# Cutting the first weight load in two, and loading x and c by their eight real rows, in a decode step that streams 165 MB

## The chip, the cores and the metric

The kernel runs on one core of a Trainium2 chip. A core has a matrix engine (TensorE, "PE" in the profile, with its weight loads as "PEld"), a vector engine (VectorE, "DVE"), a scalar engine (ScalarE, "ACT"), GpSimd ("POOL") and SyncE ("SP"), and 16 DMA engines that move data between the chip's main memory and the core's tile memory of 128 rows (partitions). SP and ACT both issue DMAs here, each on a queue of its own (q1 for SP and q10 for ACT in the profile). The metric is device time in microseconds (us) from start to end of the program: 394.66 us before, the median of three runs (394.59 to 395.08).

## The reference

One decode step of a transformer block for a batch of 8 with adaptive layer norm. `x` and `c` are both 8 rows of 512 numbers; the rest are weights and a key and value cache, all in 32-bit floats:

```
mod = (silu(c) @ w_mod).reshape(8, 6, 1, 512)         # w_mod: 512 x 3072
sa, ca, ga, sb, cb, gb = six parts of mod
h = layernorm(x) * (1 + ca) + sa
x = x + ga * attention(h, k_cache, v_cache, wq, wo)   # last 2048 keys of 8192
h = layernorm(x) * (1 + cb) + sb
x = x + gb * mlp(h, w1, b1, w2, b2)                   # relu squared, 512 -> 1792 -> 512
```

The attention has 32 query heads of 128 numbers on 8 key/value heads. For each of the 8 batch rows and 8 heads, 2048 keys and 2048 values of 128 floats are read: 134 MB of the 165 MB in all.

## The kernel before, in words

**Loads.** Nearly everything passes through five big tiles in the tile memory: four of 128 rows by 8192 floats ("big", 4096 KB each) and one half as wide ("small"). The list `loads` fixes the order: `w_mod` in two pieces (mod 0 into a big tile and mod 1 into the small one), `wq` in two, K 0, K 1, and then a K and a V piece in turn, with `wo` in between, and `w1` and `w2` last. `pump()` issues the next load of the list on SP's queue as soon as a tile of its size is free, and `done(...)` frees a tile after its last reader and calls `pump()` again. Mod 0, mod 1, wq 0, wq 1 and K 0 need no tile to come free, so they are all issued at the start; K 1 waits until the matmuls on mod 0 (L270) have let go of its tile, K 2 for those on wq 0 (L296), and so on. Each load is one DMA whose row r of 128 goes to row r of the tile. The branch for `w_mod` is at L113 to L116; a row of mod 0 is 8192 floats in one piece, 32 KB.

**x and c.** The host lays x and c out as one array of 128 x 2 x 128: the 512 columns in four groups q, each at rows 32q to 32q+7 for the eight batch rows, and zeros in the other 24 rows of each group. L64 loads it on ACT's queue, 128 rows of 1 KB, into `xc_in`.

**The head.** silu of c (L193 to L196, on ACT and DVE) and its transpose give `cT` (L189, L198). Layer norm's sums go over `xc_in` (L214 to L228) and PE adds up the four groups with the matrix `sel` (L216, L223). Then PE does `cT` times mod 0 and mod 1 (L270), DVE finishes h (L281 on), PE does the queries (L296, L311).

**The main loop** runs 32 steps over K and V pieces: DVE transposes keys (L182), PE makes scores (L351), softmax runs on ACT and DVE, PE adds up values (L440). **The tail** is the projection, the second norm and the MLP with `w1` (L603) and `w2` (L622), and the store of the output (L632).

The order on each engine is that of the program text (a manual schedule), and every engine runs its list in order. Waits are on semaphores that are placed automatically. DMAs take their completion semaphores in rotation from a set of eight, and a DMA that takes one whose last user is still under way waits for that user first.

Of the kernel before, what the change touches and what calls it, by code (L numbers as in the profile page):

```python
# [19 lines left out]
def tile_adaln_cached_attention_mlp(  # L20
# [14 lines left out]
    nc = tc.nc  # L35
    P = 128
    B, HKV, SK, DH = k_cache.shape
    D = wq.shape[0]
# [22 lines left out]

    xc_in = consts.tile([P, 2, P], F32, name="xc_in")
    x_in, c_in = xc_in[:, 0, :], xc_in[:, 1, :]
    nc.scalar.dma_start(xc_in, xc)  # L64

    ident = consts.tile([P, P], F32, name="ident")
    make_identity(nc, ident)
# [7 lines left out]
    big = NJ * DH  # L75
# [8 lines left out]
    def size_of(key):  # L84
        return "small" if key[0] in ("wo", "w1") or key == ("mod", 1) else "big"

    def load(key):
        kind, i = key
        held[key] = free[size_of(key)].pop(0)
        t = slots[size_of(key)][held[key]]  # L90
        if kind in "KV":

            hk, c = divmod(i, 2)
            v = k_cache[4 * c : 4 * c + 4, hk] if kind == "K" else v_cache[c::2, hk]
            v = v[:, SK - W :, :].rearrange("u (p j) d -> p u (j d)", j=NJ)
            cuts = (0, big // 2, big * 3 // 4, big) if key == ("V", 2 * HKV - 1) else (0, big)
            for x, y in zip(cuts, cuts[1:]):
                nc.sync.dma_start(t[:, x:y], v[..., x:y])
            return

        def rows(o, v):
            n = v.shape[1] * v.shape[2]
            nc.sync.dma_start(t[:, o : o + n].rearrange("p (a n) -> p a n", n=v.shape[2]), v)

        def wo_rows(j):

            r = 2 * REP * DH
            return wo[j * r : (j + 1) * r, :].rearrange("(h p i) n -> p h (i n)", p=P, i=4)

        w1v = w1.rearrange(r_kc, p=P)  # L110
        if kind == "wo":
            rows(0, wo_rows(i))
        elif kind == "mod":  # L113

            v = w_mod.rearrange("(p kc) n -> p (kc n)", p=P)
            nc.sync.dma_start(t, v[:, big:] if i else v[:, :big])  # L116
        elif kind == "wq":

            nc.sync.dma_start(t, wq.rearrange("(p h a) n -> h p (a n)", p=P, h=2)[i])
        elif kind == "tail":  # L120
            for h in range(2):
                rows(h * 4 * D, wo_rows(HKV // 2 - 1)[:, h : h + 1])
            rows(big // 2, w1v[:, 0:2])
        elif kind == "w1":
            rows(0, w1v[:, 2:4])
        else:
            v = w2.rearrange("(p c) n -> p c n", p=P)
            for lo, hi in ((0, 8), (8, 10), (10, 12), (12, 13), (13, 14)):
                rows(D * lo, v[:, lo:hi])
# [14 lines left out]
    def pump():  # L144
        while at[0] < len(loads) and free[size_of(loads[at[0]])]:
            load(loads[at[0]])
            at[0] += 1
# [356 lines left out]
    for s in range(N + PV_LAG + 1):  # L504
        g, i = divmod(s, C)
        q, h = divmod(s, 2)
        v = s - PV_LAG
# [104 lines left out]
    r = work.tile([P, FC, B], F32, name="relu", tag="a", bufs=1)  # L612
# [56 lines left out]
```

## Time and profile before

| what | value |
|---|---|
| median of three runs | 394.66 us |
| span of the profiled execution | 392.6 us |
| moved by DMA | 165.12 MB, mean 421 GB/s |
| PE busy | 256.3 us, 65% of the span |
| DVE busy | 218.1 us, 56% |
| ACT busy | 46.1 us, 12% |

The profiled execution is given by its span alone, from its first to its last recorded instruction; the median of the runs is 2.1 us above it, which is what lies around the span and the spread between executions. Times in rows of the profile count from the span's start. "DMA share" in a table of windows is the time of the packets that began in the window, over the 16 DMA engines, so a short window can show more than 1. A releaser in a row ("idle <- X") is what ended an engine's wait.

### The profile page before, as it was taken

The numbers are of one execution on the slowest core, as the hardware profiler recorded it, in microseconds if no ns is written. First come the engines' busy times: TensorE is split into PE (matmuls) and PEld (weight loads), VectorE is DVE, ScalarE is ACT, GpSimd is POOL, SyncE is SP. The second block draws the span as 40 slices with busy tenths as digits, with TensorE's granted clock in tenths as the row PEclk, the third lists the DMA queues.
The fourth block names the chain that finished last, engine by engine and source line by source line (L and its number), as shares of the span: only waits on it lengthen the run. The fifth ranks groups of instructions, "written<-read, shape, count | busy, mean of one in ns | idle before, by whom it ended". The sixth has DMA issues, their size and how long they took to land.

```text
span 392.6 us, 4672 instructions
## 1 busy us (share of the span) xinstructions
PE 256.3 (65%) x2006; PEld 80.7 (21%) x2006; DVE 218.1 (56%) x322; ACT 46.1 (12%) x89; POOL 1.3 (0%) x8
## 2 busy tenths in 40 slices
PE   0173869668328873797375827883775837994996
PEld 0121200122002321133021202220222211332433
DVE  1370299959056845774582817780776457855231
ACT  1200101410003100310031003010201003004010
POOL 0000000000000000000000000000000000000000
PEclk9999789988958995989699888997788959897899
DMA  8999999999999999999999999999999999999994
GB/s 329 432 425 436 444 437 437 431 426 402 454 427 427 426 427 431 429 441 430 437 423 431 427 436 427 429 431 431 407 447 427 436 431 438 426 419 412 428 423 169
DMA packets 7908, 165.12 MB, mean 421 GB/s; under 512 B 840, under 2 KB 1104, under 8 KB 1616
## 3 DMA queue, kind: packets, MB, share of 16 engines
q1 hardware_dynamic: 7728, 164.70, 98.2%
q8 instruction: 15, 0.25, 0.3%
q10 hardware_dynamic: 160, 0.14, 0.1%
q14 instruction: 5, 0.04, 0.0%
HBM read 164.77 MB, written 0.07 MB: 420 GB/s over the span
## 4 chain that ended last, share of the span: by engine, by line
DMA 65%; DVE 17%; PE 13%; issue 4%; SPq 0%; DVEq 0%
DMA big<-in_A_k_cache_dram 47%; DVE kT L182 9%; DMA big<-in_A_wq_dram 7%; DMA big<-in_A_wo_dram 6%; DMA big<-in_B_w_dram 5%; PE s_ps L351 5%; DVE pT L419 4%; PE p_ps L384 3%; PE o_ps L440 2%; DVE pr L412 2%; DVE mx L365 1%; PE m_ps L296 1%; PE m_ps L367 1%; PE m_ps L389 1%; DVE o_sb L458 1%
## 5 line engine op out<-in xcount | busy, mean ns | idle before, releaser
L182 DVE STREAM_TRANSPOSE kT<-big 128x1024 f32<-128x1024 f32 x128 | 151.7, 1221 | 90.2 <-DMA big<-in_A_k_cache_dram 86.1
L351 PE MATMUL s_ps<-kT,qst 128*32 128x512 f32 x512 | 130.1, 1076 | 19.8 <-DVE kT L182 19.7
L440 PE MATMUL o_ps<-big,pT 128*32 128x256 f32 x1024 | 73.0, 410 | 2.1 <-DMA big<-in_A_v_cache_dram 1.1
L440 PEld LDWEIGHTS o_ps<-big,pT 128*32 128x32 f32 x1024 | 35.3, 120 | 85.0 <-issue 69.5
L367 PE MATMUL m_ps<-ident,mx 128*1 128x128 f32 x16 | 4.3, 365 | 59.9 <-DVE mx L365 59.9
L351 PEld LDWEIGHTS s_ps<-kT,qst 128*32 128x32 f32 x512 | 16.4, 118 | 38.4 <-DVE kT L182 28.4
L419 DVE STREAM_TRANSPOSE pT<-pr 128x2048 f32<-128x2048 f32 x8 | 18.2, 2273 | 1.0 <-ACT pr L402 1.0
L402 ACT ACTIVATE pr<-pr,own 128x512 f32<-128x512 f32 x16 | 17.8, 1218 | 0.3
L396 ACT ACTIVATE pr<-p_ps,nm 128x512 f32<-128x512 f32 x8 | 5.5, 688 | 95.9 <-DVE nm L393 95.9
L339 ACT COPY qst<-q_ps 32x128 f32<-32x128 f32 x32 | 8.2, 257 | 72.0 <-PE q_ps L328 71.7
L361 ACT COPY ss<-s_ps 128x512 f32<-128x512 f32 x8 | 4.7, 586 | 99.5 <-issue 71.4
L296 PE MATMUL m_ps<-big,h1T 128*32 128x512 f32 x64 | 10.1, 790 | 8.5 <-DMA big<-in_A_wq_dram 8.5
L464 PE MATMUL m_ps<-o_sb,pick 128*128 128x256 f32 x16 | 6.1, 466 | 14.4 <-DVE o_sb L458 14.4
L367 PEld LDWEIGHTS m_ps<-ident,mx 128*1 128x1 f32 x16 | 0.7, 80 | 65.1 <-DVE mx L365 65.1
L314 DVE COPY qbd<-m_ps 32x128 f32<-32x128 f32 x8 | 3.0, 372 | 18.1 <-PE m_ps L311 18.0
L384 PE MATMUL p_ps<-ss,perm 128*128 128x512 f32 x16 | 11.9, 839 | 0.0
L216 PE MATMUL m_ps<-xsum,sel 128*128 128x1 f32 x2 | 0.6, 363 | 16.9 <-DVE xsum L214 16.9
L393 DVE COPY nm<-m_ps 128x1 f32<-128x1 f32 x8 | 1.3, 158 | 18.5 <-PE m_ps L389 18.5
L412 DVE TENSOR_SCALAR pr<-pr,own 128x512 f32<-128x512 f32 x16 | 9.2, 654 | 0.8 <-ACT pr L396 0.8
L457 DVE TENSOR_SCALAR o_sb<-o_ps,bit 128x128 f32<-128x128 f32 x16 | 4.9, 306 | 7.7 <-PE o_ps L440 7.7
L423 PE MATMUL m_ps<-zs,tsel 128*128 128x8 f32 x16 | 2.9, 252 | 8.9 <-DVE zs L414 8.9
L464 PEld LDWEIGHTS m_ps<-o_sb,pick 128*128 128x128 f32 x16 | 2.6, 203 | 25.9 <-DVE o_sb L458 25.9
(124 smaller groups left out, 119.8 us busy)
## 6 DMA issues: line engine op xcount, KB each, us to landing
big<-in_A_k_cache_dram SPq DMA_DIRECT2D x16, 4096.0 KB, 28.8
big<-in_A_v_cache_dram SPq DMA_DIRECT2D x15, 4096.0 KB, 20.9
big<-in_A_wq_dram SPq DMA_DIRECT2D x2, 4096.0 KB, 32.1
small<-in_A_wo_dram SPq DMA_DIRECT2D x3, 2048.0 KB, 26.6
big<-in_w_mod_dram SPq DMA_DIRECT2D x1, 4096.0 KB
small<-in_w_mod_dram SPq DMA_DIRECT2D x1, 2048.0 KB, 17.1
big<-in_A_v_cache_dram SPq DMA_DIRECT2D x1, 2048.0 KB, 21.5
big<-in_A_v_cache_dram SPq DMA_DIRECT2D x2, 1024.0 KB, 21.2
```

The costliest lines, as they stand in the source:

```text
L182: nc.vector.transpose(KTS[q, j][:, rows], k[:, rows, 32 * j : 32 * j + 32])
L296: nc.tensor.matmul(pqs[r][32 * g : 32 * g + 32, :], hT[:, kc, :], w[:, 4 * r + g, :], start=(kc == 0), stop=(kc == NQ - 1),)
L339: nc.scalar.copy(own[b, :, :, i, 0], pq[b, :P].rearrange("p (c m t) -> p c m t", c=2, t=REP))
L351: nc.tensor.matmul(s_ps[0][32 * g : 32 * g + 32, :], qst[hk % 2][:, P * (4 * c + u) + 32 * j :][:, :32], kT[:, u], start=(c == 0 and j == ...
L367: nc.tensor.matmul(MX_[hk][0:1, :P], mx, ident, start=True, stop=True)
L384: nc.tensor.matmul(sp, perm, SS_.pop(hk), start=True, stop=True)
L396: nc.scalar.activation(pr.rearrange("p j x -> p (j x)"), SS_.pop(hk), AF.Exp, bias=nm, scale=SCALE, accum_out=z)
L402: nc.scalar.mul(X_[hk][..., w], pr, own[:, w : w + 1])
L412: nc.vector.tensor_scalar(X_[hk][..., w], pr, own[:, w : w + 1], None, op0=ALU.mult)
L419: nc.vector.transpose(PT_[hk].rearrange("p e j r -> p j e r"), X_.pop(hk).rearrange("p j x w -> p j (x w)"))
L440: nc.tensor.matmul(O_[n][32 * g : 32 * g + 32, : 2 * DH], PT_[hk][:, e, j : j + 2].rearrange("p j r -> p (j r)"), vt[:, j : j + 2, :].rear ...
L464: nc.tensor.matmul(pp[:, : 2 * DH], pick.rearrange("p t u -> p (t u)"), o.rearrange("p e d -> p (e d)"), start=True, stop=True)
```

## The change

Two edits. The load of x and c becomes a clearing of the whole tile on DVE and then four DMAs of 8 rows each, on the same queue as before. The load of mod 0 becomes two DMAs on SP's queue, of its first 16 rows and of the other 112; mod 1 stays one DMA.

```diff
     xc_in = consts.tile([P, 2, P], F32, name="xc_in")
     x_in, c_in = xc_in[:, 0, :], xc_in[:, 1, :]
-    nc.scalar.dma_start(xc_in, xc)
+    nc.vector.memset(xc_in, 0.0)
+    for q in range(D // P):
+        nc.scalar.dma_start(xc_in[32 * q : 32 * q + B], xc[32 * q : 32 * q + B])
...
             v = w_mod.rearrange("(p kc) n -> p (kc n)", p=P)
-            nc.sync.dma_start(t, v[:, big:] if i else v[:, :big])
+            for r in (slice(0, P),) if i else (slice(0, 16), slice(16, P)):
+                nc.sync.dma_start(t[r], v[r, big:] if i else v[r, :big])
```

In the lists of instructions that the two programs build, SP has one DMA more, ACT three more and DVE one memset more, ahead of all its other work. The rotation of the eight semaphores moves by four places. That places new waits near the start: on SP, the load of wq 1 waits until the 16-row piece has landed, and that of K 0 until the first load of x and c has; on ACT, the load of the activation table ahead of L193 waits for the other three loads of x and c, and all four of these wait for the memset. From K 1 on, each load waits for the same earlier loads as before or for ones of the start, and in the tail every wait has its counterpart.

## The prediction

> **What bounds the kernel now.** I read the page first, for the share of DMA, then the table of windows by stage, then the start in order of time, then the last links of the chain.
>
> ```profile
> span 392.6 us, 4672 instructions
> ...
> PE 256.3 (65%) x2006; PEld 80.7 (21%) x2006; DVE 218.1 (56%) x322; ACT 46.1 (12%) x89; POOL 1.3 (0%) x8
> ...
> q1 hardware_dynamic: 7728, 164.70, 98.2%
> q8 instruction: 15, 0.25, 0.3%
> q10 hardware_dynamic: 160, 0.14, 0.1%
> ...
> DMA 65%; DVE 17%; PE 13%; issue 4%; SPq 0%; DVEq 0%
> ```
>
> No engine is busy over 65%, but SP's queue q1 keeps all 16 DMA engines at work for 98.2% of the span. Its rate is 164.70 MB over 16 x 392.6 x 0.982 us = 26.7 GB/s for one engine, so a 32 KB row of mod 0 costs an engine 32,768 / 26,700 = 1.23 us. The next table (time, busy time of each engine, clock, DMA share, GB/s) shows whether the stream ever pauses.
>
> ```profile
> 1.50:3.50 2.00, 0.00 (x0) 0.00 (x0) 0.75 (x6) 0.96 (x1) 0.00 (x0) 1.00 0.96 262
> 3.50:12.50 9.00, 0.00 (x0) 0.00 (x0) 0.00 (x0) 0.00 (x0) 0.00 (x0) 1.00 0.98 421
> 12.50:42.00 29.50, 15.78 (x116) 5.35 (x120) 10.55 (x42) 2.88 (x7) 0.00 (x0) 0.93 1.03 441
> 42.00:384.00 342.00, 235.37 (x1779) 72.14 (x1772) 205.95 (x271) 41.98 (x81) 0.47 (x1) 0.86 1.00 429
> 384.00:392.60 8.60, 5.14 (x116) 3.19 (x114) 0.60 (x3) 0.00 (x0) 0.00 (x0) 1.00 0.35 135
> ```
>
> From 1.5 us to 384 us it doesn't: the share is 0.96 to 1.03 in each stretch. The chain's last links say that the end follows the last load at once:
>
> ```profile
> 346.09 22.87 DMA big<-in_A_wo_dram
> ...
> 369.03 19.87 DMA big<-in_B_w_dram
> ...
> 388.94 0.47 PE m_ps L622 x8
> ```
>
> So the span is a start of about 1.75 us, one unbroken stream, and some 4 us behind it. Whatever makes the stream start earlier, shrinks it or slows it anywhere moves the end by as much; what compute does early is covered as long as SP issues each load before the stream has used up those ahead of it. That cover is large at the start:
>
> ```profile
> 0.73 0.42 ACTq L64 DMA_DIRECT2D xc_in<-in_xc_dram  x1
> ...
> 0.73 0.39 SPq L116 DMA_DIRECT2D big<-in_w_mod_dram  x1
> ...
> 1.18 0.42 SPq L116 DMA_DIRECT2D small<-in_w_mod_dram  x1
> 1.18 1.28 ACT L193 ACT_TABLE_LOAD   x1 [1.18 <-PEq L655]
> ...
> 13.54 0.31 ACT L193 ACTIVATE e_sb<-xc_in 128x128 f32<-128x128 f32 x1 [11.08 <-DMA xc_in<-in_xc_dram]
> ...
> 18.80 6.40 PE L270 MATMUL m_ps<-big,cT 128*32 128x512 f32 x40
> ```
>
> ```profile
> 25.27 0.54 SPq L98 DMA_DIRECT2D big<-in_A_k_cache_dram  x1
> ```
>
> ```profile
> DMA to landing us min/median/max: 33.2/35.5/46.1
> ```
>
> The last row is for L98's first loads: K 0, issued at 2.68 us, is the longest, 46.1 us, and lands at 48.8 us. K 1 is issued at 25.27 us, when the tile of mod 0 is free. The head could thus run 48.8 - 25.3 = 23.5 us later before the stream stood still, and running earlier gains nothing.
>
> **The 16-row piece.** How rows and engines go together is seen in half-microsecond windows (same columns):
>
> ```profile
> 1.00:1.50 0.50, 0.00 (x0) 0.00 (x0) 0.17 (x1) 0.32 (x1) 0.44 (x2) 1.00 0.00 0
> 1.50:2.00 0.50, 0.00 (x0) 0.00 (x0) 0.40 (x3) 0.50 (x1) 0.00 (x0) 1.00 2.73 721
> 2.00:2.50 0.50, 0.00 (x0) 0.00 (x0) 0.35 (x3) 0.46 (x1) 0.00 (x0) 1.00 0.73 197
> 2.50:3.00 0.50, 0.00 (x0) 0.00 (x0) 0.00 (x0) 0.00 (x0) 0.00 (x0) 1.00 0.37 131
> 3.00:3.50 0.50, 0.00 (x0) 0.00 (x0) 0.00 (x0) 0.00 (x0) 0.00 (x0) 1.00 0.00 0
> 3.50:4.00 0.50, 0.00 (x0) 0.00 (x0) 0.00 (x0) 0.00 (x0) 0.00 (x0) 1.00 1.29 545
> 4.00:4.50 0.50, 0.00 (x0) 0.00 (x0) 0.00 (x0) 0.00 (x0) 0.00 (x0) 1.00 1.25 537
> ```
>
> What begins from 1.5 to 3.0 us is 0.5 x (721 + 197 + 131) = 524 KB, 16 rows of 32 KB, one on each engine; then nothing until the next 16 rows at 3.5 to 4.5 us. A 128-row load is thus 16 equal streams of 8 rows each. The 16-row piece gives all 16 engines one row each, too, but all of them in one corner of the tile. If the ways into the tile memory belong to rows, as the even split of 128 rows over 16 streams suggests but doesn't show, these 16 rows share few ways. Bounds: with 16 ways the piece takes 1.23 us, as before; with eight neighbouring rows to a way it has two ways and takes 8 x 1.23 = 9.84 us, a loss of 8.6 us. No row here shows a load of few rows with weight, so I choose between the ends: four ways, in the lower half of the steps 2, 4, 8, 16, because the simplest cut of 128 rows into 16 streams keeps neighbours together. That is 4 x 1.23 = 4.92 us, a loss of **3.7 us** (an estimate; 0 to 8.6). Behind it on each engine stand its rows of the 112-row piece, so nothing covers the loss.
>
> [...]
>
> **The 112 rows.** Seven rows to an engine, 7 x 1.23 = 8.6 us if they never meet. But 112 rows no longer fall on the ways in the even pattern: with 16 ways of 8 rows, the ways that the first piece left alone have 8 rows to take, 9.84 us, so 1.2 us is lost even if all runs smoothly; at worst an engine stands behind another one's row four times, 4 x 1.23 = 4.9 us. Without shared ways it is 0. I take **1.2 us**, since the streams queue ahead and can even out.
>
> **An earlier start.** The first wave is slow: from 1.5-2.0 to 3.5-4.0 us is 2.0 us instead of 1.23, and the sixteen rows begin up to a microsecond apart. If that comes from SP setting up 128 rows at once, a small first piece takes up to 0.8 us off; if it is the delay of the first read, nothing. Part of it would vanish under the sharing. I take **0.4 us gained** (0 to 0.8).
>
> **x and c.** 96 of 128 packets of 1 KB go. q10's 160 packets cost 0.1% of the span, 0.4 us on each engine, x and c being most of it. Four DMAs of 8 rows put at most four packets on one engine, where eight were: half is gained where the packets remain, **0.2 us** (0 to 0.4). [...]
>
> The memset lies between these prices on DVE:
>
> ```profile
> L260 DVE MEMSET qbd<- 128x1024 f32 x1 | 0.9, 912 | 0.2 <-issue 0.2
> ...
> L255 DVE MEMSET pick<- 128x128 f32 x1 | 0.2, 165 | 0.0
> ```
>
> On the line through the two, 128x256 takes 165 + 128 x 747 / 896 = 272 ns. DVE then is free at about 1.1 us, before `sel` needs it (1.33 us, when POOL has made `ident`). ACT's first DMA waits for it, and four issues of 0.42 us end near 2.9 us. c comes by four packets an engine instead of eight, each behind a row of mod 0, so it could land some 4 x 1.25 = 5 us sooner, and under the sharing at about the old time; the table load of 1.28 us, which was under the wait, now follows it. All this is in the head, with its cover of 23.5 us: **0 us**. Without the cover it would be the 1.28 us.
>
> **SP's list.** One issue more, 0.39 us, moves mod 1, wq 0 and those behind them; the stream has 9.8 us of mod 0 by then: 0. wq 1 now waits for the 16-row piece (about 7 us) and K 0, queued behind wq 1, for the first x/c load (about 14 us at worst). Ahead of wq 1 are 10 MB, which last until 1.75 + 8 x 1.23 + 4 x 1.23 + 8 x 1.23 = 26 us: 0, and if the x/c load came after 26 us the stream would pause for the difference.
>
> **The sum.** 3.7 + 1.2 - 0.4 - 0.2 = +4.3 us, 396.9 us of span against 392.6, and with the median of the runs 394.66 + 4.3 = **399.0 us**.
>
> **The rivals.** *No shared ways.* The 16 engines write the corner at full rate, because the limit is the engine and not the row. For it: each engine's 26.7 GB/s explains every row above by itself. Against it: nothing here, since no load with weight goes to few rows. Then the savings stand alone, 394.66 - 0.6 = 394.1 us, 393.4 at the ends of both; faster. It decides as soon as the sharing costs under 0.6 us.
>
> *Rows dealt in turn.* If the engines take the 112 rows one by one in turn, each of the eight waves stands in 16 neighbouring rows and takes 4.92 us: 8 x (4.92 - 1.23) = 29.5 us, 424 us. Against it: streams that each stay in their part are the easier reading of 16 even streams.
>
> *SP starved.* If x and c, on few engines and behind stalled rows, landed ten microseconds after the 26 us at which the queue is used up, K 0 and all behind it would be ten late: 409 us with the sharing. Against it: x and c landed at 13.5 us behind eight rows and now wait for four.
>
> **How the numbers follow.** Forecast 0.71, no shared ways 0.23, rows in turn 0.03, SP starved 0.03. The forecast's own range is from 396.3 (eight ways, +1.2, the 112 rows +1.2, savings of 0.8) to 403.3 us (+3.7, +4.9, no savings). About 0.8 us, 0.2%, is what a measurement of this kernel can tell from no change. Within the second case I give 0.11 to a gain over that, and 0.12 to less. So faster 0.11, same 0.12, slower 0.77. The range runs from 394.0, which leaves about 0.1 below, to 403.3, which leaves about 0.1 above.
>
> **What would show it.** In the profile after: half-microsecond windows in which, behind the first 524 KB, little begins for some 5 us (right) or the next wave comes within 2 us (no shared ways); a rate in the first 20 us well under 400 GB/s; L270's first matmul released by a load of `w_mod` and not by ACT; later windows at 429 GB/s as before; the wait for x and c ended by 14 us; and the last load landing as much later as the span grew. The forecast is wrong if the second wave is prompt, or if the first stretch is slow and a later one wins it back.

## The result, and the profile after

The changed kernel takes 404.35 us (median of 5 runs, 403.75 to 404.79) against 394.59 us for the one before in the same comparison (median of 5, 394.35 to 395.08): a ratio of 1.0244, with a 95% interval of 1.0232 to 1.0257. That is 9.8 us slower where 4.3 us slower was forecast, and outside the range. The profiled execution's span went from 392.6 to 402.0 us, by 9.4 us.

From the page of the changed kernel (span; busy time of the engines; the DMA queues with packets, MB and share of 16 engines; the chain of work by engine):

```profile
span 402.0 us, 4681 instructions
...
PE 255.7 (64%) x2006; PEld 79.5 (20%) x2006; DVE 218.2 (54%) x323; ACT 46.1 (11%) x89; POOL 1.3 (0%) x8
...
q1 hardware_dynamic: 7744, 164.70, 98.2%
...
q10 hardware_dynamic: 80, 0.04, 0.1%
...
DMA 65%; DVE 18%; PE 13%; issue 3%; ACT 1%; ACTq 0%; POOL 0%; DVEq 0%; POOLq 0%; SPq 0%
```

The engines do the same work in the same time (PE 255.7 us and 256.3 before, DVE 218.2 and 218.1), and q1 carries the same 164.70 MB at the same share of a longer span: its packets themselves took longer. Where is seen in windows of the changed kernel (time, busy time of each engine, clock, DMA share, GB/s):

```profile
1.50:6.50 5.00, 0.00 (x0) 0.00 (x0) 0.76 (x6) 0.00 (x0) 0.00 (x0) 1.00 1.37 211
6.50:22.00 15.50, 0.00 (x0) 0.00 (x0) 0.00 (x0) 0.00 (x0) 0.00 (x0) 1.00 0.89 223
22.00:42.00 20.00, 12.54 (x100) 4.38 (x100) 10.50 (x42) 4.16 (x8) 0.00 (x0) 1.00 1.01 430
...
```

```profile
42.00:384.00 342.00, 229.54 (x1749) 68.94 (x1746) 202.30 (x258) 41.19 (x78) 0.47 (x1) 0.86 1.00 429
```

Until 22 us the rate is about half of the 421 GB/s of the kernel before; from then on it is that of before, 429 GB/s. All of the loss lies in the load of mod 0, which ends some 9.5 us later, and the last load and the end come later by about as much (9.3 and 9.4 us). The chain's last wait for a load of `w2` began at 369.03 us before the change, and now reads:

```profile
378.34 19.83 DMA big<-in_B_w_dram
```

In half-microsecond windows the start reads:

```profile
1.50:2.00 0.50, 0.00 (x0) 0.00 (x0) 0.41 (x3) 0.00 (x0) 0.00 (x0) 1.00 4.88 721
2.00:2.50 0.50, 0.00 (x0) 0.00 (x0) 0.35 (x3) 0.00 (x0) 0.00 (x0) 1.00 0.00 0
2.50:3.00 0.50, 0.00 (x0) 0.00 (x0) 0.00 (x0) 0.00 (x0) 0.00 (x0) 1.00 2.33 328
3.00:3.50 0.50, 0.00 (x0) 0.00 (x0) 0.00 (x0) 0.00 (x0) 0.00 (x0) 1.00 0.00 0
3.50:4.00 0.50, 0.00 (x0) 0.00 (x0) 0.00 (x0) 0.00 (x0) 0.00 (x0) 1.00 0.00 0
4.00:4.50 0.50, 0.00 (x0) 0.00 (x0) 0.00 (x0) 0.00 (x0) 0.00 (x0) 1.00 0.58 70
...
6.00:6.50 0.50, 0.00 (x0) 0.00 (x0) 0.00 (x0) 0.00 (x0) 0.00 (x0) 1.00 3.67 660
```

The 16-row piece begins between 1.5 and 3.0 us, 0.5 x (721 + 328) = 524 KB as before the change; but then the next rows begin only from 4 us on, most of them after 6 us, where the kernel before began its second wave at 3.5 to 4.5 us. The small first piece brought no earlier first byte, and x and c came late:

```profile
22.95 1.28 ACT L196 ACT_TABLE_LOAD   x1 [22.95 <-DMA xc_in<-in_xc_dram]
...
29.51 5.91 PE L273 MATMUL m_ps<-big,cT 128*32 128x512 f32 x36
```

ACT waits for them until 22.95 us, not 13.54, and the first matmul on mod 0 starts at 29.51 us instead of 18.80. The stream doesn't feel it: SP issues K 1 at 35.92 us, and the DMA share stays at 1.01 in the window from 22 to 42 us.

```profile
35.92 0.54 SPq L100 DMA_DIRECT2D big<-in_A_k_cache_dram  x1
```

### The profile page after: what moved, and what is told of

It reads as the page before. It is cut to its first block, busy times and chain, and to the rows that moved or that the text cites. A ratio compares the mean times of both kernels' runs of the same rounds, so it can differ in the third digit from the quotient of the medians.

```text
span 402.0 us, 4681 instructions
## 1 busy us (share of the span) xinstructions
PE 255.7 (64%) x2006; PEld 79.5 (20%) x2006; DVE 218.2 (54%) x323; ACT 46.1 (11%) x89; POOL 1.3 (0%) x8
## 3 DMA queue, kind: packets, MB, share of 16 engines
q1 hardware_dynamic: 7744, 164.70, 98.2%
## 4 chain that ended last, share of the span: by engine, by line
DMA 65%; DVE 18%; PE 13%; issue 3%; ACT 1%; ACTq 0%; POOL 0%; DVEq 0%; POOLq 0%; SPq 0%
DMA big<-in_A_k_cache_dram 49%; DVE kT L185 8%; PE s_ps L354 6%; DMA big<-in_A_wo_dram 6%; DMA xc_in<-in_xc_dram 5%; DMA big<-in_B_w_dram 5%; DVE pT L422 3%; PE o_ps L443 2%; PE p_ps L387 2%; DVE pr L415 1%; PE m_ps L299 1%; DVE mx L368 1%; DVE o_sb L461 1%; DVE qst L263 0%; PE m_ps L370 0%
## 5 line engine op out<-in xcount | busy, mean ns | idle before, releaser
L299 PE MATMUL m_ps<-big,h1T 128*32 128x512 f32 x64 | 9.1, 721 | 7.1 <-DMA big<-in_A_wq_dram 6.0
```

The lines of the kernel that those rows point to most:

```text
L299: nc.tensor.matmul(pqs[r][32 * g : 32 * g + 32, :], hT[:, kc, :], w[:, 4 * r + g, :], start=(kc == 0), stop=(kc == NQ - 1),)
```

## The experiments

### One part of the change at a time

The edit of x and c alone:

```diff
-    nc.scalar.dma_start(xc_in, xc)
+    nc.vector.memset(xc_in, 0.0)
+    for q in range(D // P):
+        nc.scalar.dma_start(xc_in[32 * q : 32 * q + B], xc[32 * q : 32 * q + B])
```

> Only the edit of x and c. If the whole loss of 9.8 us comes from cutting mod 0 by rows (theory A), this kernel is within 0.5 us of the one before, 394.1 to 394.7 us, and x and c land near 13.5 us. If the new waits or the few-row loads of x and c cost by themselves (theory B), it is slower than before by 1 us or more.

Measured: 394.36 us against 394.56, ratio 0.9995 (0.9987 to 1.0004): no difference. x and c landed no earlier than in the kernel before (waits of ACT; engine, line, releaser, us in total, times, longest):

```profile
ACT L195 <- DMA xc_in<-in_xc_dram: 14.0, 1, 14.0
```

The cut of mod 0 into 16 and 112 rows alone:

```diff
-            nc.sync.dma_start(t, v[:, big:] if i else v[:, :big])
+            for r in (slice(0, P),) if i else (slice(0, 16), slice(16, P)):
+                nc.sync.dma_start(t[r], v[r, big:] if i else v[r, :big])
```

> Only the cut of mod 0 into 16 and 112 rows. Theory A (the cut by rows): 404.0 to 405.0 us, all of the loss, with the first 15 us of the stream under 300 GB/s. Theory B (x and c): no more than 399 us.

Measured: 403.86 us against 394.56, ratio 1.0232 (1.0218 to 1.0245); the interval overlaps that of the whole change. Rates in the same profile:

```profile
4.00:8.00 4.00, 0.00 (x0) 0.00 (x0) 0.00 (x0) 0.00 (x0) 0.00 (x0) 1.00 0.95 164
8.00:12.00 4.00, 0.25 (x2) 0.25 (x2) 2.81 (x11) 0.31 (x1) 0.00 (x0) 1.00 1.02 262
12.00:16.00 4.00, 0.93 (x4) 0.76 (x4) 1.38 (x9) 2.04 (x4) 0.00 (x0) 1.00 1.02 262
```

Here PE and DVE are at work by 12 us, as x and c come early (ACT begins on c at 8.4 us), and the time is lost all the same. So theory A holds: the cut by rows is the loss, and the late x and c are not.

### Other cuts of mod 0

By columns, 1024 and 7168 of all 128 rows:

```diff
-            nc.sync.dma_start(t, v[:, big:] if i else v[:, :big])
+            for x, y in ((big, big * 3 // 2),) if i else ((0, 1024), (1024, big)):
+                nc.sync.dma_start(t[:, x % big : x % big + y - x], v[:, x:y])
```

> Mod 0 cut by columns instead of rows: all 128 rows of the first 1024 columns, then all 128 rows of the other 7168. The first piece has 524 KB as in the changed kernel. If a small first piece starts the stream earlier, up to 0.8 us faster than before (393.8 to 394.6 us); if any cut of the load costs, slower. If the loss comes from which rows a load covers, no loss here.

Measured: 394.65 us against 394.56, ratio 1.0000 (0.9991 to 1.0008). A cut as such costs nothing, and a first piece of 524 KB doesn't gain anything either. Its windows, of an execution with a span of 394.3 us, show the first bytes at the old time and no more of them:

```profile
1.50:3.50 2.00, 0.00 (x0) 0.00 (x0) 0.76 (x6) 0.96 (x1) 0.00 (x0) 1.00 0.85 182
3.50:12.50 9.00, 1.18 (x4) 1.01 (x4) 3.67 (x16) 2.35 (x5) 0.00 (x0) 1.00 1.04 440
```

Into rows 0 to 63 and 64 to 127 (the edit is shown against the cut into 16 and 112 rows, here and in the next one):

```diff
-            for r in (slice(0, P),) if i else (slice(0, 16), slice(16, P)):
+            for r in (slice(0, P),) if i else (slice(0, 64), slice(64, P)):
```

> Mod 0 cut into rows 0 to 63 and 64 to 127, so that each engine has a regular four rows of each piece. [...] Theory A2 (the loss comes from the corner of 16 rows and from seven rows to an engine, which fit no even pattern): at most 396 us.

Measured: 405.32 us against 394.56, ratio 1.0267 (1.0253 to 1.0280), 10.8 us more. A2, at most 396 us, falls: 64 rows to a piece, four for each of the 16 engines, don't help when they lie in one half of the tile. The rate through mod 0 was half of the 421 GB/s before:

```profile
4.00:22.00 18.00, 1.17 (x4) 1.00 (x4) 8.30 (x36) 2.04 (x4) 0.00 (x0) 1.00 1.00 206
```

Into the 64 even and the 64 odd rows:

```diff
-            for r in (slice(0, P),) if i else (slice(0, 16), slice(16, P)):
+            for r in (slice(0, P),) if i else (slice(0, P, 2), slice(1, P, 2)):
```

> Mod 0 cut by rows again, but into the 64 even and the 64 odd rows, so that each piece has four rows on each of 16 ways. If the loss of the cut by rows is only that the rows of a piece crowd on some ways, this cut costs nothing: 394.0 to 395.2 us, against 405.3 us for rows 0 to 63 and 64 to 127. If any cut by rows costs, over 396 us.

Measured: 394.59 us against 394.63, ratio 0.9996 (0.9987 to 1.0004): no loss. The same number of rows and bytes in a piece costs 10.8 us or nothing, by which rows they are.

```profile
3.50:12.50 9.00, 1.18 (x4) 1.01 (x4) 5.69 (x31) 2.04 (x4) 0.00 (x0) 1.00 0.95 408
```

### One piece at a time, in mid-stream

To price each piece away from the start, one more load was put behind mod 0, into rows of the tile that K 0 overwrites before anything reads it. All of mod 0 is loaded by one DMA, as before the change, so the output is computed in full.

```diff
             nc.sync.dma_start(t, v[:, big:] if i else v[:, :big])
+            if i == 0:
+                nc.sync.dma_start(slots["big"][3][0:16], v[:16, :big])
```

> The kernel before with one more load, straight behind mod 0 in SP's queue: 16 rows of 32 KB of w_mod into rows 0 to 15 of the tile that K 0 fills later (nothing reads them). Its bytes alone are 1.23 us of the stream. [...] Theory E (the engine is the limit and the row does not matter): 395.8 us.

Measured: 399.58 us against 394.81, 4.8 us more (ratio 1.0124, 1.0109 to 1.0139). With rows `0:P:8` in place of `0:16`:

> The same additional load, but into rows 0, 8, 16 to 120, every eighth. [...] Theory F (any load of few rows is slow, wherever the rows lie): the same as for rows 0 to 15. Theory E: 395.8 us.

Measured: 397.58 us against 394.81, 2.8 us more (1.0075, 1.0058 to 1.0092). Theory E (395.8 us) falls with both, and theory F, the same time for both, with the second; the prediction's four ways, 4.9 us for rows 0 to 15, fit the first. Both loads read the same 16 rows of `w_mod`, so the difference lies in the rows of the tile. The windows of rows 0 to 15, and then of every eighth row:

```profile
12.50:13.50 1.00, 0.00 (x0) 0.00 (x0) 0.00 (x0) 0.00 (x0) 0.00 (x0) 1.00 3.77 507
13.50:15.50 2.00, 0.00 (x0) 0.00 (x0) 0.00 (x0) 0.22 (x1) 0.00 (x0) 1.00 0.00 0
15.50:17.50 2.00, 0.00 (x0) 0.00 (x0) 1.78 (x4) 0.09 (x1) 0.00 (x0) 1.00 0.81 107
```

```profile
12.50:13.50 1.00, 0.00 (x0) 0.00 (x0) 0.00 (x0) 0.00 (x0) 0.00 (x0) 1.00 2.11 507
13.50:14.25 0.75, 0.00 (x0) 0.00 (x0) 0.00 (x0) 0.00 (x0) 0.00 (x0) 1.00 0.00 0
14.25:16.00 1.75, 0.00 (x0) 0.00 (x0) 1.10 (x2) 0.31 (x1) 0.00 (x0) 1.00 0.80 197
```

Nothing new begins for two microseconds in the first, and little for two more; in the second the gap is 0.75 us. The share of the first window, 3.77 against 2.11, is the time that these packets took: 3.77 x 16 = 60 us for 507 KB, some 15.5 rows, so 3.9 us for a row, against 2.2 us in the second and the 1.23 us of a row in the stream. The 112 rows with `16:P`, and the source rows `v[:112]`:

> The same with 112 rows, into rows 16 to 127: the second piece of the changed kernel's cut by itself. Evenly spread its bytes are 8.6 us, 403.2 us. With the fullest ways as the limit (eight rows each) 9.8 us, 404.4 us. If it goes at the pace of the changed kernel's first 20 us, 262 GB/s, it takes 3.67 MB / 262 = 14.0 us, 408.6 us: then 5.4 us of the loss belong to the 112 rows and not to the 16.

Measured: 409.67 us against 394.81, 14.9 us more (1.0378, 1.0359 to 1.0397), where its bytes are 8.6 us: 6.3 us are lost by the 112 rows.

```profile
12.50:26.50 14.00, 7.50 (x44) 2.73 (x44) 7.81 (x34) 2.35 (x5) 0.00 (x0) 1.00 1.02 262
```

That is 1.02 x 16 x 14 / 112 = 2.0 us for a row instead of 1.23. The loss isn't a stall in one place: in the two-microsecond windows from 14 to 26 us the mean row takes 1.7 to 2.3 us, and the fastest of them is

```profile
18.00:20.00 2.00, 1.00 (x4) 0.92 (x4) 0.32 (x2) 0.94 (x3) 0.00 (x0) 1.00 0.96 295
```

With rows `0:112`:

> An additional load behind mod 0 again, 112 rows into rows 0 to 111 instead of 16 to 127 (which cost 14.9 us). If the start at row 16 was the trouble, under 12 us more than before; if seven rows to an engine are, again 13 to 16 us, 408 to 411 us. By the fullest way alone, 9.8 us, 404.5 us.

Measured: 409.95 us against 394.63, 15.3 us more (1.0385, 1.0366 to 1.0404). Not the start at row 16. With rows `0:96`, six for each engine, 3.15 MB or 7.4 us when evenly spread:

> [...] By the fullest way: 9.8 us, 404.5 us. If the writes of the moment crowd as with 112 rows (1.7 times the even time): 12.6 us, 407.3 us.

Measured: 409.39 us against 394.63, 14.8 us more (1.0367, 1.0348 to 1.0385), twice the 7.4 us of its bytes, and more than either expectation. Over six rows it is 2.5 us for a row, 2 x 1.23 us. The trace shows such a pace: from 14.3 us on 16 rows begin (477 GB/s x 1.10 us = 525 KB), then nothing for 1.45 us, then 16 more. With as many rows as engines, the share times the window is the mean time of a row: 2.33 x 1.10 = 2.6 us and 2.07 x 1.10 = 2.3 us.

```profile
14.30:15.40 1.10, 0.00 (x0) 0.00 (x0) 1.02 (x2) 0.01 (x1) 0.00 (x0) 1.00 2.33 477
15.40:16.85 1.45, 0.00 (x0) 0.00 (x0) 1.31 (x8) 0.00 (x0) 0.00 (x0) 1.00 0.00 0
16.85:17.95 1.10, 0.57 (x2) 0.50 (x2) 0.47 (x3) 0.00 (x0) 0.00 (x0) 1.00 2.07 477
```

With the 64 rows `0:P:2`, four for each engine and, if they lie evenly, four for each of the 16 ways of eight rows that the prediction assumed:

> [...] If only the total of rows per way counts: 4 x 1.23 = 4.9 us, 399.5 us. [...]

Measured: 399.58 us against 394.81, 4.8 us more (1.0122, 1.0105 to 1.0139), its bytes and nothing else:

```profile
12.50:17.25 4.75, 0.13 (x1) 0.13 (x1) 2.81 (x11) 0.31 (x1) 0.00 (x0) 1.00 1.02 437
```

So the bytes, at the rate of the stream, are enough to price this load. They aren't for 96 and 112 neighbouring rows: they took 14.8 and 14.9 us, where the author's estimate from the fullest way, with eight rows, was 9.8 us. Which engine takes which row of such a load, in which order, and which rows share a way, no row of the profile shows, and it stays open.

## Why the prediction was wrong

**What bounds the kernel** was right: no engine's work changed, the stream slowed in one place, and the end moved by as much.

**The 16-row piece** was right, place and size: 3.7 us were forecast from four ways, and the piece alone costs 4.8 us of which 1.23 us are its bytes, 3.5 us. Every eighth row, as many rows and bytes, costs 2.8 us. The choice of four ways among 2, 4, 8 and 16 could have gone otherwise by the rows alone, so that the size fits is in part luck. The ways themselves, how many there are and which rows go together, no run shows: they were the author's assumption. What the runs show is rates by rows: mod 0 in rows 0 to 63 and 64 to 127 ran at 206 GB/s, the even and odd rows at 408, 96 neighbouring rows at 213 and 112 at 262.

**The 112 rows** are the step that failed: "I take 1.2 us, since the streams queue ahead and can even out". They don't even out. The piece alone loses 14.9 - 8.6 = 6.3 us, more than even the 4.9 us set as the worst. The 1.2 us came from an estimate of the rows per way, and the worst case from one engine's bad luck, both on the assumption of 16 ways of eight rows, which no run shows; the measured pace is 262 GB/s, against 16 x 26.7 = 427 at the rate of the stream, and a row takes 2.0 us on average from beginning to end. That is 14.9 us where the estimate has 9.8; what the rows lose the rest to, stays open. The two pieces lose 3.5 + 6.3 = 9.8 us, which is the measured loss, 9.8 us. Each term is known to 0.6 to 0.8 us only, the sum takes it that the two simply add, and the cut by itself lost 9.3 us, so the match to a tenth is partly chance.

**The earlier start** of 0.4 us did not come. The cut by columns, which has a small first piece and loses nothing by it, gains nothing either (1.0000), and the first bytes come between 1.5 and 2.0 us with and without it; so here the bytes of the first load didn't matter. That piece still has all 128 rows. Half as many rows don't help either: q1's 16 rows from 1.5 to 3.5 us, in the kernel before and in the cut into even and odd rows, read

```profile
q1 hardware_dynamic: 16, 0.52, 95.6%
```

```profile
q1 hardware_dynamic: 16, 0.52, 96.0%
```

which is 0.96 x 2.0 = 1.9 us for a first row in both. What makes the first wave slow stays open.

**x and c**: 0.2 us of gain were forecast, and 0.2 us is the difference of the medians in the run of this edit alone, within its interval. The landing was wrong: "5 us sooner", or about the old time under the sharing, was forecast, and alone it was 14.0 us against 13.54, in the changed kernel 22.95. The queue's count shows what came in: 96 packets of data fewer should leave 64 of 160, and 80 are there, 16 more. In the first 45 us, q10 has 144 packets before the change and 64 after it: 16 beyond the 128 rows of the one load, and 32 beyond the 32 rows of the four. So the rows of data fell to a quarter, and the packets to less than a half. How they are spread over the engines no row shows. The trace of this edit alone shows their pace. From 7 to 8 us, and then from 8 to 9.5 us:

```profile
q1 hardware_dynamic: 16, 0.52, 121.3%
q10 hardware_dynamic: 8, 0.00, 0.5%
```

```profile
q1 hardware_dynamic: 16, 0.52, 80.9%
q10 hardware_dynamic: 8, 0.01, 1.5%
```

Beside 16 rows of mod 0 go eight packets of under 512 bytes each, and beside the next 16 rows eight packets of 1 KB. At eight packets to 16 rows, 64 packets last for 8 x 1.23 = 9.8 us, as long as the 128 rows of mod 0 (an estimate); so the small ones took up what the rows of data had saved. In the changed kernel a row takes longer, 0.89 x 16 x 15.5 / 105 = 2.1 us by its window from 6.5 to 22 us, and at the same pace, 8 x 2.1 = 17 us, x and c come late. Packets of q10 don't always go at this pace: in the run of the cut of mod 0 alone, x and c ran between 4 and 8 us, beside 16 rows of mod 0 (164 GB/s x 4 us = 656 KB, 524 + 131). Why they were faster there, the runs don't show. Two of the prediction's signs failed with the landing: the wait for x and c did not end by 14 us, and PE's first matmul on mod 0 came straight behind the sums over x (L226) and not behind a load of `w_mod`.

**SP's new waits** cost nothing, as forecast: the share is 1.04 from 8 to 12 us, with K 0 issued at 8.58 us, and 1.01 from 22 to 42 us, with K 1 at 35.92. The cover shrank only a little: K 1 was issued at 35.92 us instead of 25.27, 10.7 us later (9.4 us from x and c, 1.28 us from the table load behind them), and the stream is itself late by some 9.5 us.

**The rivals.** No shared ways (whose low end is 394.66 - 1.2 = 393.5 us and not 393.4) is refuted by x16 in its two forms (4.8 and 2.8 us for the same bytes) and by the two cuts into 64 rows (10.8 us and none). Rows dealt in turn, 424 us, was not met, but was nearer to the truth in one thing: the loss goes through the whole load and not only through its first piece (262 GB/s over the 112 rows).

## What to carry to other kernels

In a kernel like this one, whose DMA stream never pauses, a load's rows can decide its speed as much as its bytes: here a cut by neighbouring rows halves the rate of the pieces (206 GB/s, 10.8 us on 4 MB, for rows 0 to 63 and 64 to 127), while a cut by columns, or into even and odd rows, costs nothing. Before a load is cut by rows, both pieces are to be priced, the large remainder too; here it lost 6.3 of 9.8 us. And before a start is split for an earlier first byte, the trace should show what the first byte waits for: here neither fewer bytes nor fewer rows in the first load brought it forward.

## What the runs showed of the hardware that was not expected

A load of 112 neighbouring rows runs at 262 GB/s and one of 96 rows takes 14.8 us for 3.15 MB, 213 GB/s, though both numbers divide by 16, and the rows of the second were seen to begin 16 at a time; 64 rows taken every second reach 437 GB/s. Four loads of 8 rows on a second queue landed no sooner beside 32 KB rows (14.0 us) than one load of four times the bytes (13.54 us).
